# Expert matmuls on two 64-row tiles with two accumulations open at once, in an attention and mixture-of-experts kernel

## The chip, the cores and the metric

The kernel runs on one core of one Trainium2 chip. The metric is the device time of one execution in microseconds (us). Five engines work side by side: the TensorE (PE, with its weight loads shown apart as PEld), the VectorE (DVE), the ScalarE (ACT), GpSimd (POOL) and the SyncE (SP), whose queue issues most of the DMAs.

## The reference

What must be computed is attention with one key and value head for all sixteen query heads, followed by a mixture of experts with a choice in two stages. Cut to what matters:

```python
batch, n_heads, seq, head_dim = (8, 16, 384, 64)
scores = scale * np.matmul(q, k.transpose(0, 1, 3, 2))
attn = softmax(scores)
attn_out = np.matmul(attn, v)                       # (8, 16, 384, 64)
x = attn_out.transpose(0, 2, 1, 3).reshape(3072, 1024)
g_idx = argmax(x @ w_group)                         # 4 groups
e_idx = argmax(x_g @ w_expert[g])                   # 4 experts in a group
h = relu(x_e @ w1[g, e])                            # 1024 x 1024
out[tokens] = (g_w * e_w)[:, None] * (h @ w2[g, e]) # 1024 x 1024
```

All 384 tokens of a batch have nearly the same x, since the attention is nearly uniform, so that in seven of the eight batches all tokens go to one expert; in the last one 363 go to one and 21 to another.

## The kernel before

The work is cut into 96 steps. A step handles two units of two heads each, for one tile of 128 queries. Four steps make a tile t, three tiles (twelve steps) make a batch; this document calls these twelve steps a cycle and numbers the steps of a cycle 0 to 11, so step 16 of the program is step 4 of its cycle. The order in which each engine works is written out by hand: what an engine is given in the loop over `i` is what it does, in that order.

In each step:

- `scores` puts the scores of two units into PSUM. Each unit is two fp32 matmuls of 64 rows, one on the upper and one on the lower half of the array, into a bank each. Two such pairs of banks exist, so a unit waits until ACT has done with the same unit of the step before.
- `soft` lets DVE take the maximum (`nmx`) and ACT the exponential (`pr`) with its sum; `norm` lets DVE take the reciprocal and POOL multiply; `transp` lets DVE transpose the probabilities of the step before last into `ring`.
- In the steps with `p` 2 and 3 of a tile, `pv` multiplies with V for the tile before, on 32-row tiles into four banks `x`; after `p` 3, `pv_out` lets ACT copy the four banks to `xt`, and POOL cast them into the bf16 `xb`, from which the experts read.
- In the steps with `p` 0 and 1, the TensorE works on an expert. `expert` is a generator; `advance(groups)` lets it go on by so many accumulations of eight matmuls of 128 rows.

Besides, `logits` computes the logits of both stages on 32-column tiles, from the fp32 `xt`: for tile 0 of a batch in step 8 of its cycle, for tiles 1 and 2 in step 4 of the next. `logits_out` and `gate_masks` (DVE, one step later) turn them into masks. `gate_choose` counts, in a matmul with ones, for which expert the tokens of tile 0 vote, and `gate_pick` and `load_main` fetch the winner's weights (four DMAs that cast to bf16, issued by POOL in step 10). The expert of a batch begins in step 5 of the next cycle. Tokens that chose another expert are found at the end: the last batch has a second expert by plan, and a loop over a count read on the chip would run whatever is left.

All short-lived accumulations (pv, logits, the count, the experts) share four banks that `xbank()` gives out in turn; who takes a bank waits for whoever read it last. After the last step the score banks serve the experts too (`bank_end`).

The matmuls of an expert are 64 of 384 columns (`w1`, line 440, then a relu by ACT on line 446) and 48 of 512 columns (`w2`, line 454, then a scaled copy by ACT on line 472, and the stores by SP on line 498).

Of the kernel before, what the change touches and what calls it, by code (L numbers as in the profile page):

```python
# [19 lines left out]
def kernel(  # L20
# [11 lines left out]
    nc = tc.nc  # L32
    B, H, S, D = q.shape
# [5 lines left out]
    ST = S // P  # L39
    KO = Dm // P  # L40
    FO = F // P
    GE = G * Eg
# [25 lines left out]
    ident = singles.tile([P, P], FP32)  # L68
    make_identity(nc, ident)

    blank = singles.tile([P, 512], BF16)
    nc.vector.memset(blank[:], 0.0)

# [10 lines left out]
    st = {}  # L84
# [125 lines left out]
    def transp(u):  # L210

        nc.vector.transpose(  # L212
            out=ring[:, (u // 4) % 3, u % 4].rearrange("p h s -> p (h s)"),
            in_=st.pop(("pr", u))[:].rearrange("p h s -> p (h s)"),
        )
# [89 lines left out]
    def gate_choose(b):  # L305

        mask = st["g", b][1]
        c_ps = xbank()
        nc.tensor.matmul(
            out=c_ps[:, 0:GE], lhsT=ones[:], rhs=mask[:, 0].rearrange("p g e -> p (g e)"), start=True, stop=True  # L310
        )
        st["c_ps", b] = c_ps

# [116 lines left out]
    def keep_xb(b):  # L430
        nc.sync.dma_start(out=xb_dram[b], in_=st["xb", b][:].rearrange("p c t -> p (c t)"))

    def expert(xb, w1, w2, result, psum, on_act=None):

        on_act = on_act or (lambda k: k % 2 == 0)
        h_t = pool.tile([P, FO, S], BF16, tag="hT", bufs=1)
        for fc in range(FO):
            hp = psum()
            for ko in range(KO):
                nc.tensor.matmul(  # L440
                    out=hp[:, 0:S], lhsT=w1[:, ko, ts(fc, P)], rhs=xb[:, ko, :], start=(ko == 0), stop=(ko == KO - 1)
                )
                if ko % (KO // 2) == KO // 2 - 1:
                    yield
            if on_act(fc):
                nc.scalar.activation(out=h_t[:, fc, :], in_=hp[:, 0:S], func=ACTF.Relu)  # L446
            else:
                nc.vector.tensor_scalar(out=h_t[:, fc, :], in0=hp[:, 0:S], scalar1=0.0, scalar2=None, op0=ALU.max)
            yield
        for j in range(ST):  # L450
            for nh in range(2):
                yp = psum()
                for fo in range(FO):
                    nc.tensor.matmul(  # L454
                        out=yp, lhsT=h_t[:, fo, ts(j, P)], rhs=w2[:, fo, ts(nh, 512)],
                        start=(fo == 0), stop=(fo == FO - 1),
                    )
                    if fo % (FO // 2) == FO // 2 - 1:
                        yield
                result(j, nh, yp, on_act(FO + 2 * j + nh))  # L460
                yield

    def scaled(gcol, store):

# [60 lines left out]
    NT = B * ST  # L525
    pending = []

    def advance(groups):
        for _ in range(3 * groups):
# [19 lines left out]
    for b in range(B):  # L549
        s0 = SB * b  # L550
        for x, j0, j1 in ((s0 + 8, 0, 1), (s0 + 16, 1, ST)):
            at(x, "m2", logits, b, j0, j1)
            at(x + 1, "v", logits_out, b, j0, j1)
        for x, j0, j1 in ((s0 + 9, 0, 1), (s0 + 17, 1, ST)):
            at(x, "v", lambda b=b, j0=j0, j1=j1: st.__setitem__(("gm", b), gate_masks(b, j0, j1)))
            at(x, "v", lambda b=b: [next(st["gm", b]) for _ in range(3)])
        if b == 0:
            at(s0 + 10, "s", gate_choose, b)
            at(s0 + 10, "b", gate_score, b)
        else:  # L560
# [52 lines left out]
    load_v(0)  # L613
    for i in range(NSL):
        t, p = i // 4, i % 4
        if i >= SB + 5 and (i - 5) % SB == 0:
            pending.append(main_expert((i - 5) // SB - 1, lambda k: True))
        us = (2 * i, 2 * i + 1)
        for u in us:
            scores(u)  # L620
        run(i, "s")
        soft(us, lambda: run(i, "b"))
        if p < 2:
            run(i, "m0")
# [12 lines left out]
        run(i, "e")  # L637
        if p == 3 and t > 0:
            pv_out(t - 1)
        run(i, "g")  # L640
# [5 lines left out]
    st["ended"] = True  # L646
    transp(2 * i - 4)
    transp(2 * i - 3)
    advance(2)
    transp(2 * i - 2)  # L650
    transp(2 * i - 1)
    advance(2)
    run(i + 1, "w")
    advance(1)
    pv(NT - 1, 0, NB)
    pv_out(NT - 1)
    load_second(0)
    advance(2)
    run(i + 4, "m2")
    run(i + 4, "g")  # L660
    pending.append(main_expert(b, lambda k: k < FO or k % 2 == 0))
    advance(1)
# [102 lines left out]
```

## Time and profile before

| what | value |
|---|---|
| median of three runs | 530.9 us (530.18 to 537.23) |
| profiled execution | 532.53 us, its span 530.8 us |
| mean granted TensorE clock | 0.989 |
| TensorE busy | 502.5 us, 95% of the span |
| VectorE busy | 425.5 us, 80% |
| ScalarE busy | 319.2 us, 60% |
| GpSimd busy | 273.6 us, 52% |
| HBM | 101.79 MB read, 18.87 MB written |

A row of the timeline has the start, the length, the engine, the line, the operation, output<-inputs, shapes and count. `64*128` is the shape of the array's tile, rows by columns. The record of a matmul ends when its last result has left the array, so that the records of matmuls that follow each other overlap; the time of one is the distance between starts. An fp32 matmul stands as two rows. In brackets is the idle time of the engine ahead of the row, and what ended it.

### The profile page before, as it was taken

Reading aid. Unit: us, or ns where it says so; the run is one execution under the profiler, and the core shown is the slowest. Engines: PE = TensorE matmul, PEld = TensorE weight load, DVE = VectorE, ACT = ScalarE, POOL = GpSimd, SP = SyncE. Lnnn points to the kernel's source line nnn. Section 1 sums busy time; section 2 is a strip of 40 time slices with the busy share of each in tenths; the row PEclk is TensorE's granted clock in tenths of the full one; section 3 lists DMA queues with packets and bytes.
Section 4 is the critical chain, followed back from the end, with each engine's and each line's share of the span. In section 5 each row is a group of like instructions: output and inputs, shape, how many; then the busy total and the mean of one; then the engine's idle time right before and its main releaser. Section 6 shows DMA issues by size and latency. Waiting matters only on the chain.

```text
span 530.8 us, 18465 instructions
## 1 busy us (share of the span) xinstructions
PE 502.5 (95%) x7450; PEld 283.2 (53%) x7466; DVE 425.5 (80%) x825; ACT 319.2 (60%) x1005; POOL 273.6 (52%) x464
## 2 busy tenths in 40 slices
PE   6787899999999999999999999999999999999993
PEld 2254455555566556645555556645665555555451
DVE  2899988898899879998899878997999789914221
ACT  3676666677666766676576766676766666623210
POOL 1656854575565654485457546475358535613000
PEclk9799999999999999999999999999999999999998
DMA  7522699349963998379963996399946980199953
GB/s 119 123 43 43 122 239 217 72 82 224 262 151 63 212 250 226 72 125 237 272 133 61 223 251 166 72 186 233 270 81 105 232 232 2 26 230 259 212 117 96
DMA packets 64998, 84.14 MB, mean 159 GB/s; under 512 B 20496, under 2 KB 39952, under 8 KB 64912
## 3 DMA queue, kind: packets, MB, share of 16 engines
q0 software_dynamic: 19008, 37.75, 39.7%
q1 hardware_dynamic: 44720, 44.74, 32.1%
q8 instruction: 60, 0.98, 0.7%
q10 hardware_dynamic: 1184, 0.45, 0.4%
q14 instruction: 26, 0.21, 0.1%
HBM read 101.79 MB, written 18.87 MB: 227 GB/s over the span
## 4 chain that ended last, share of the span: by engine, by line
PE 79%; DVE 8%; DMA 6%; ACT 2%; issue 2%; POOL 1%; ACTq 0%; POOLq 0%; DVEq 0%
PE s L180 23%; PE x L228 23%; PE x L440 13%; PE x L454 12%; DMA w<-in_moe_w_dram 5%; PE sb L454 4%; DVE nmx L188 4%; DVE ring L212 3%; ACT pr L191 2%; PE sb L440 2%; PE x L251 2%; POOL pr L206 1%; DMA q_sb<-in_q_dram 1%; POOL w L415 0%; DVE rinv L202 0%
## 5 line engine op out<-in xcount | busy, mean ns | idle before, releaser
L206 POOL TENSOR_SCALAR pr<-pr,rinv 128x384 f32<-128x384 f32 x384 | 217.4, 586 | 193.8 <-DVE rinv L202 193.7
L191 ACT ACTIVATE pr<-s,nmx 128x384 f32<-128x384 f32 x384 | 217.7, 578 | 139.3 <-DVE nmx L188 131.5
L188 DVE TENSOR_REDUCE nmx<-s 128x2 f32<-128x768 f32 x192 | 174.0, 944 | 43.5 <-PE s L180 42.9
L212 DVE STREAM_TRANSPOSE ring<-pr 128x768 f32<-128x768 f32 x192 | 175.2, 951 | 0.1
L180 PE MATMUL s<-kt,qt 64*128 64x384 f32 x768 | 156.2, 520 | 11.8 <-ACT pr L191 11.7
L228 PE MATMUL x<-ring,v_sb 32*64 32x256 f32 x4608 | 140.1, 379 | 3.9 <-issue 2.8
L228 PEld LDWEIGHTS x<-ring,v_sb 32*64 32x64 f32 x4608 | 101.9, 131 | 45.7 <-issue 26.4
L180 PEld LDWEIGHTS s<-kt,qt 64*128 64x128 f32 x768 | 66.6, 189 | 71.9 <-ACT pr L191 36.0
L440 PEld LDWEIGHTS <-w 128*128 128x128 bf16 x576 | 54.5, 98 | 46.0 <-issue 11.4
L191 ACT ACTIVATION_READ_ACCUMULATOR pr<-s,nmx 128x1 f32 x384 | 77.8, 203 | 0.0
L440 PE MATMUL x<-xb,w 128*128 128x384 bf16 x448 | 76.4, 326 | 0.0
L454 PEld LDWEIGHTS <-h_t 128*128 128x128 bf16 x432 | 40.6, 98 | 56.9 <-issue 10.5
L454 PE MATMUL x<-w,h_t 128*128 128x512 bf16 x276 | 64.6, 380 | 0.6
L242 ACT COPY xt<-x 128x256 f32<-128x256 f32 x96 | 28.8, 392 | 8.9 <-PE x L228 8.9
L454 PE MATMUL sb<-w,h_t 128*128 128x512 bf16 x140 | 31.7, 379 | 0.3
L243 POOL CAST xb<-xt 128x1024 bf16<-128x1024 f32 x24 | 24.8, 1035 | 11.3 <-ACT xt L242 11.3
L446 ACT ACTIVATE h_t<-x 128x384 bf16<-128x384 f32 x56 | 25.2, 502 | 6.4 <-PE x L440 3.6
L415 POOL DMA_DIRECT2D w<-in_moe_w_dram x36 | 27.6, 780 | 0.3 <-issue 0.3
L170 DVE STREAM_TRANSPOSE qt<-q_sb 128x512 f32<-128x512 f32 x38 | 25.9, 682 | 0.0
L472 ACT ACTIVATE y<-x,gsel 128x512 f32<-128x512 f32 x36 | 24.3, 696 | 2.3 <-PE x L454 2.3
L440 PE MATMUL sb<-xb,w 128*128 128x384 bf16 x128 | 21.4, 326 | 0.0
L202 DVE RECIPROCAL rinv<-ssum 128x4 f32<-128x4 f32 x96 | 13.8, 144 | 3.1 <-ACT pr L191 3.1
(79 smaller groups left out, 139.3 us busy)
## 6 DMA issues: line engine op xcount, KB each, us to landing
w<-in_moe_w_dram POOLq DMA_DIRECT2D x36, 1024.0 KB, 19.5
q_sb<-in_q_dram SPq DMA_DIRECT2D x76, 224.0 KB, 6.3
out_dram<-y SPq DMA_DIRECT2D x84, 128.0 KB, 6.6
xb_scratch<-xb SPq DMA_DIRECT2D x8, 768.0 KB, 5.0
v_sb<-in_v_dram SPq DMA_DIRECT2D x32, 96.0 KB, 4.5
kk<-in_k_dram SPq DMA_DIRECT2D x30, 92.0 KB, 5.4
q_sb<-in_q_dram SPq DMA_DIRECT2D x16, 128.0 KB, 3.4
out_dram<-y SPq DMA_DIRECT2D x24, 64.0 KB, 1.7
```

Of the source, the lines that this page charges most:

```text
L170: nc.vector.transpose(out=qt[:].rearrange("p (x d) -> p x d", d=32), in_=q_sb[:, :, 0:32])
L180: nc.tensor.matmul(out=s[:, h, 0:S], lhsT=qt[r, ts(cc, P)], rhs=kt[r, :], start=True, stop=True)
L188: nc.vector.tensor_reduce(out=nmx[:], in_=s[:, :, 0:S], axis=AX.X, op=ALU.max, negate=True)
L191: nc.scalar.activation(out=pr[:, h, :], in_=s[:, h, 0:S], func=ACTF.Exp, bias=nmx[:, h:h + 1], scale=1.0, accum_out=ssum[:, k, h:h + 1],)
L206: nc.gpsimd.tensor_scalar(out=pr, in0=pr, scalar1=rinv[:, k, h:h + 1], scalar2=1.0, op0=ALU.mult, op1=ALU.mult)
L212: nc.vector.transpose(out=ring[:, (u // 4) % 3, u % 4].rearrange("p h s -> p (h s)"), in_=st.pop(("pr", u))[:].rearrange("p h s -> p (h s)"),)
L228: nc.tensor.matmul(out=o[i][h * D:(h + 1) * D, 0:2 * P].rearrange("d (g c q) -> d g c q", g=2, c=4), lhsT=v_sb[r, n, :], rhs=ring[r, a:z + ...
L242: nc.scalar.copy(out=xt[:, :, ts(i, 32)], in_=o[:, 0:2 * P].rearrange("p (c q) -> p c q", c=KO))
L415: nc.gpsimd.dma_start(out=w[:, o:o + 4, :], in_=(w1f, w2f)[n][ds(e, 1), :, o:o + 4, :].rearrange("o p c f -> (o p) c f"))
L440: nc.tensor.matmul(out=hp[:, 0:S], lhsT=w1[:, ko, ts(fc, P)], rhs=xb[:, ko, :], start=(ko == 0), stop=(ko == KO - 1))
L446: nc.scalar.activation(out=h_t[:, fc, :], in_=hp[:, 0:S], func=ACTF.Relu)
L454: nc.tensor.matmul(out=yp, lhsT=h_t[:, fo, ts(j, P)], rhs=w2[:, fo, ts(nh, 512)], start=(fo == 0), stop=(fo == FO - 1),)
```

## The change

The eight matmuls of 128 rows of one accumulation become sixteen matmuls of 64 rows. Two accumulations (a pair) are open at once, in two banks: for each of the eight slices of the contraction, the upper 64 rows go to one bank and the lower 64 rows to the other. That is one phase. In a second phase of the same pair the two halves change banks. Between the two phases of a pair stands a fence: a memset of one column on DVE that waits for the last matmul of the first phase, and for which the first matmul of the second phase waits. `fence()` is called right behind the scores of a step for all pairs that are open, and for one pair in the middle of a step where both its phases lie in that step.

An expert is fourteen phases in a fixed order, in which two pairs alternate: pairs 0 to 3 are `w1`, pairs 4 to 6 `w2`. `advance(phases)` now counts phases. They are spread as two in each of steps 4, 5, 8 and 9, and three in each of steps 0 and 1; before, the accumulations were spread as two in step 4, three in 5, two in 8, three in 9 and two in each of 0 and 1, of which those of step 4 belonged to the expert of the batch before. So an expert now begins in step 4 (step 16 of the program for the first) and ends in step 1. The logits come ahead of the expert's matmuls in steps 4 and 8 and are transposed in the same step. The count for the choice takes the 64 tokens in the lower partitions of tile 0 in place of 128. `bank_end` gives the two banks of a tile one after the other.

```diff
-            out=c_ps[:, 0:GE], lhsT=ones[:], rhs=mask[:, 0].rearrange("p g e -> p (g e)"), start=True, stop=True
+            out=c_ps[:, 0:GE], lhsT=ones[0:64, :], rhs=mask[0:64, 0].rearrange("p g e -> p (g e)"),
...
+    def fence(pairs=None):
+        pairs = list(unfenced) if pairs is None else pairs
+        if pairs:
+            f = nc.vector.memset(mark[:], 0.0)
+            tc.add_manual_dep(f.ins, [unfenced.pop(x) for x in pairs][-1].name, after, reason="banks change row tiles")
+            fenced.update(dict.fromkeys(pairs, f.ins))
...
-        for fc in range(FO):
-            hp = psum()
-            for ko in range(KO):
-                nc.tensor.matmul(
-                    out=hp[:, 0:S], lhsT=w1[:, ko, ts(fc, P)], rhs=xb[:, ko, :], start=(ko == 0), stop=(ko == KO - 1)
-                )
...
+        def phase(pair, swap):
+            ms = (2 * pair, 2 * pair + 1)
+            operands, n = (first, S) if ms[0] < FO else (second, 512)
+            if not swap:
+                banks[pair] = [psum() for _ in ms]
+            for c in range(KO):
+                for r in range(2):
+                    lhsT, rhs = operands(ms[r ^ swap], c, slice(64 * r, 64 * (r + 1)))
+                    mm = nc.tensor.matmul(
+                        out=banks[pair][r ^ swap][:, 0:n], lhsT=lhsT, rhs=rhs,
+                        start=(not swap and c == 0), stop=(swap == 1 and c == KO - 1),
+                    )
+                    if swap and c == 0 and r == 0:
+                        tc.add_manual_dep(mm.ins, fenced.pop(pair).name, after, reason="banks change row tiles")
+            if not swap:
+                unfenced[pair] = mm.ins
+            if swap:
+                for m, bank in zip(ms, banks.pop(pair)):
+                    evict(m, bank)
...
+        for pair, swap in (
+            (0, 0), (1, 0), (0, 1), (1, 1), (2, 0), (3, 0), (2, 1), (3, 1),
+            (4, 0), (5, 0), (4, 1), (6, 0), (5, 1), (6, 1),
+        ):
+            if swap and pair in unfenced:
+                for x in list(unfenced) if st.get("ended") else [pair]:
+                    fence([x])
+            phase(pair, swap)
             yield
...
-            free.extend(x[:, h, :] for h in range(2) for x in sb)
+            free.extend(x[:, h, :] for x in sb for h in range(2))
...
-            at(x, "m2", logits, b, j0, j1)
-            at(x + 1, "v", logits_out, b, j0, j1)
+            at(x, "m0", logits, b, j0, j1)
+            at(x, "v", logits_out, b, j0, j1)
...
-        if i >= SB + 5 and (i - 5) % SB == 0:
-            pending.append(main_expert((i - 5) // SB - 1, lambda k: True))
+        if i >= SB + 4 and (i - 4) % SB == 0:
+            pending.append(main_expert((i - 4) // SB - 1, lambda k: True))
...
+        fence()
         soft(us, lambda: run(i, "b"))
         if p < 2:
             run(i, "m0")
-            advance(1)
             run(i, "m1")
-            advance(2 if p == 1 and t % ST > 0 else 1)
+            advance(2)
...
         if i >= 2:
             transp(2 * i - 4)
+        if p < 2 and t % ST == 0:
+            advance(1)
+        if i >= 2:
             transp(2 * i - 3)
```

After the loop the remaining phases of the seventh expert, the eighth and the second one follow in the same way, with three, two and one phases around the last pv.

More of the change, by code (lines that the diff above doesn't have):

```diff
@@ L69 @@
     make_identity(nc, ident)
+    mark = singles.tile([P, 1], FP32)
     blank = singles.tile([P, 512], BF16)
@@ L309, in gate_choose @@
         nc.tensor.matmul(
-            out=c_ps[:, 0:GE], lhsT=ones[:], rhs=mask[:, 0].rearrange("p g e -> p (g e)"), start=True, stop=True
+            out=c_ps[:, 0:GE], lhsT=ones[0:64, :], rhs=mask[0:64, 0].rearrange("p g e -> p (g e)"),
+            start=True, stop=True,
         )
@@ L431, in keep_xb @@
         nc.sync.dma_start(out=xb_dram[b], in_=st["xb", b][:].rearrange("p c t -> p (c t)"))
+    after = mybir.DependencyInfo(mybir.DependencyClass.Sync, mybir.DependencyReason.DATA)
+    unfenced, fenced = {}, {}
+    def fence(pairs=None):
[4 more added lines that the diff above has]
+            fenced.update(dict.fromkeys(pairs, f.ins))
     def expert(xb, w1, w2, result, psum, on_act=None):
@@ L436, in expert @@
         h_t = pool.tile([P, FO, S], BF16, tag="hT", bufs=1)
-        for fc in range(FO):
-            hp = psum()
-            for ko in range(KO):
-                nc.tensor.matmul(
-                    out=hp[:, 0:S], lhsT=w1[:, ko, ts(fc, P)], rhs=xb[:, ko, :], start=(ko == 0), stop=(ko == KO - 1)
-                )
[L443 to L446, printed above, removed]
-            else:
-                nc.vector.tensor_scalar(out=h_t[:, fc, :], in0=hp[:, 0:S], scalar1=0.0, scalar2=None, op0=ALU.max)
-            yield
@@ L450, in expert @@
[L450 to L461, printed above, removed]
+        banks = {}
@@ new lines, in first, with second @@
+        def first(m, c, r):
+            return w1[r, c, ts(m, P)], xb[r, c, :]
+        def second(m, c, r):
+            j, nh = divmod(m - FO, 2)
+            return h_t[r, c, ts(j, P)], w2[r, c, ts(nh, 512)]
+        def phase(pair, swap):
[17 more added lines that the diff above has]
+                    evict(m, bank)
@@ new lines, in evict @@
+        def evict(m, bank):
+            if m >= FO:
+                result(*divmod(m - FO, 2), bank, on_act(m))
+            elif on_act(m):
+                nc.scalar.activation(out=h_t[:, m, :], in_=bank[:, 0:S], func=ACTF.Relu)
+            else:
+                nc.vector.tensor_scalar(out=h_t[:, m, :], in0=bank[:, 0:S], scalar1=0.0, scalar2=None, op0=ALU.max)
+        for pair, swap in (
[6 more added lines that the diff above has]
+            phase(pair, swap)
+            yield
@@ L526, with advance @@
     pending = []
-    def advance(groups):
-        for _ in range(3 * groups):
+    def advance(phases):
+        for _ in range(phases):
             while pending:
@@ L648 @@
     transp(2 * i - 3)
-    advance(2)
+    advance(3)
     transp(2 * i - 2)
     transp(2 * i - 1)
+    run(i + 1, "w")
     advance(2)
-    run(i + 1, "w")
-    advance(1)
     pv(NT - 1, 0, NB)
@@ L657 @@
     load_second(0)
-    advance(2)
-    run(i + 4, "m2")
+    advance(1)
+    run(i + 4, "m0")
+    run(i + 4, "v")
     run(i + 4, "g")
```

## The prediction

> **What bounds the kernel now.** I read the page first, then the order of the TensorE alone over one cycle of twelve steps, then the other engines at the places where the change puts something new. On the page, the second line gives busy time and the third what the chain that ended last is made of.
>
> ```profile
> span 530.8 us, 18465 instructions
> ...
> PE 502.5 (95%) x7450; PEld 283.2 (53%) x7466; DVE 425.5 (80%) x825; ACT 319.2 (60%) x1005; POOL 273.6 (52%) x464
> ...
> PE 79%; DVE 8%; DMA 6%; ACT 2%; issue 2%; POOL 1%; ACTq 0%; POOLq 0%; DVEq 0%
> ```
>
> So the TensorE sets the time. The columns of the next view are start, length, engine, line, tiles and count. I call the visits S (scores, L180), E (expert, L440 and L454), PV (L228), L (logits, L251) and G (the choice, L309), and number the steps 0 to 11 from 228.76 on; S0 is the start of step 0.
>
> ```profile
> 228.76 1.56 PE L180 MATMUL s<-kt,qt 64*128 64x384 f32 x8
> ...
> 247.40 1.56 PE L180 MATMUL s<-kt,qt 64*128 64x384 f32 x8
> 248.89 3.63 PE L454 MATMUL x<-w,h_t 128*128 128x512 bf16 x15
> 252.45 1.10 PE L251 MATMUL x<-xt,wge 128*32 128x64 f32 x64
> 253.48 1.56 PE L180 MATMUL s<-kt,qt 64*128 64x384 f32 x8
> 254.97 4.07 PE L440 MATMUL x<-xb,w 128*128 128x384 bf16 x24
> 258.97 1.56 PE L180 MATMUL s<-kt,qt 64*128 64x384 f32 x8
> 260.46 2.85 PE L228 MATMUL x<-ring,v_sb 32*64 32x256 f32 x96
> ...
> 267.51 1.56 PE L180 MATMUL s<-kt,qt 64*128 64x384 f32 x8
> 269.00 2.77 PE L440 MATMUL x<-xb,w 128*128 128x384 bf16 x16
> 271.70 0.76 PE L251 MATMUL x<-xt,wge 128*32 128x32 f32 x64
> 272.40 1.56 PE L180 MATMUL s<-kt,qt 64*128 64x384 f32 x8
> 273.89 4.07 PE L440 MATMUL x<-xb,w 128*128 128x384 bf16 x24
> 277.80 0.17 PE L309 MATMUL x<-mask_all,ones 128*128 128x16 bf16 x1
> ```
>
> Each visit starts before the record of the last has ended, so in these steps no other engine is waited for. What is left to save is the price of changing the tile shape. Twenty-four E matmuls followed by G, of the same 128-row shape, take 277.80 - 273.89 = 3.91 us, 0.163 each. Followed by S, of 64-row shape, they take 258.97 - 254.97 = 4.00. A change of shape costs 0.09. The view of line L180 by itself (shortest, median, longest duration in ns) gives the other part:
>
> ```profile
> L180 PEld LDWEIGHTS s<-kt,qt x32: 183/186/187, 259.0 to 273.2; 64*128 64x128 f32 x32
> L180 PE MATMUL s<-kt,qt x32: 482/482/587, 259.0 to 273.5; 64*128 64x384 f32 x32
> ```
>
> The first pass of a visit is 0.105 longer than the rest: its weights have to be loaded with nothing streaming, after the change of shape. The other three passes add (1.56 - 0.587)/3 = 0.324 each, so S is 1.30 of streaming. S is also the form of the new E: two 64-row tiles at once, one bank each.
>
> **The change part by part: what it saves.** In the new kernel S, E and G all have 64 rows. Between S and E neither change remains: 0.09 into E, and 0.09 + 0.105 into the next S, 0.29 per visit in steps 0, 1, 5 and 9. In steps 4 and 8 the logits now stand between S and E, so two changes stay and only 0.09 + 0.105 goes. Sum 4 x 0.29 + 2 x 0.195 = 1.55 us per cycle, or 10 us over the six and a half cycles in which experts run. Bounds: nothing, if a bf16 tile after an fp32 tile still drains, and this 10.
>
> **The new matmuls.** Two 64-row matmuls take the place of one of 128 rows. No row shows bf16 at 64 rows. If the two tiles stream side by side, as those of S do, the cost is nothing; if one after the other, it is the whole E time again: 9 experts x 112 x about 0.186 (0.163 for 64 of them, 0.216 for the 48 of 512 columns) = 187 us. I take nothing, since the S rows are the nearest. Weight loads are twice as many, and the row of the old ones is
>
> ```profile
> L440 PEld LDWEIGHTS <-w 128*128 128x128 bf16 x576 | 54.5, 98 | 46.0 <-issue 11.4
> ```
>
> If each pair's load were in the open, that would be 9 x 112 x 0.098 = 99 us. S speaks against it: only its first load of four shows. The Trainium skill, page "TensorE: Matmul & The Clock Gate", Part 3, The mechanism, has it that a weight load overlaps a running matmul only if the two lie in different row groups. By that rule each row tile would wait for its own loads and the 99 us would be due; the S rows, where the second, third and fourth load of the same row group hide, disagree, and I go by them.
>
> **The earlier start: xb.** The expert's first pair now comes in step 4, right behind the logits, and reads the whole of xb, whose last third POOL casts in that very step:
>
> ```profile
> 247.81 2.26 POOL L206 TENSOR_SCALAR pr<-pr,rinv 128x384 f32<-128x384 f32 x4 [2.00 <-DVE rinv L202]
> 248.36 1.82 DVE L188 TENSOR_REDUCE nmx<-s 128x2 f32<-128x768 f32 x2 [0.64 <-PE s L180]
> 250.02 1.04 POOL L243 CAST xb<-xt 128x1024 bf16<-128x1024 f32 x1
> ```
>
> The cast stands behind the four normalisations and ends at 251.06, 3.66 after the step's start. The TensorE is there after S (1.30 + 0.105), a change (0.09) and L (253.48 - 252.45 = 1.03, its own change in it): 2.52. The old kernel did not care: in step 4 it still ran the previous expert. Wait 1.15 plus a handover: 1.2, in seven cycles 8.4 us. S of step 5 stands behind it. Bounds 1.0 and 1.3.
>
> **G and the h_t evictions.** The four x banks go round in turn. In step 9 the first two phases close, and G takes the bank that pair 2's first relu frees. ACT has that relu behind the step's four exponentials. The old kernel's rows for this chain:
>
> ```profile
> 272.62 0.67 DVE L170 STREAM_TRANSPOSE qt<-q_sb 128x512 f32<-128x512 f32 x1
> 273.36 1.82 DVE L188 TENSOR_REDUCE nmx<-s 128x2 f32<-128x768 f32 x2
> 275.10 0.21 DVE L261 STREAM_TRANSPOSE lg<-x 128x32 f32<-128x32 f32 x1
> 276.65 0.88 ACT L446 ACTIVATE h_t<-x 128x384 bf16<-128x384 f32 x2
> ```
>
> From the maximum to the end of the first relu it is 276.65 + 0.50 - 273.36 = 3.79 (two relus 0.88, so one is about 0.50). In the old kernel G needed no such bank. In the new step 9 the maximum starts at the earliest 0.86 after S begins to stream (272.40 to 273.36 less the 0.105), so the bank is free at 4.65; the TensorE arrives at 1.30 + 16 x 0.163 = 3.91. DVE closes step 8 with the row of 272.62, 5.78 after that step's start (267.51); with the logits' transpose (0.21) and a fence of 0.06 it is 6.05, where S of step 9 begins at 1.40 + 0.09 + 0.70 + 2.61 = 4.80 and its maximum could start at 5.66: 0.4 later. Wait 0.75 to 1.2; I take 1.1, 7.7 us in seven cycles. S of step 10 is queued behind G.
>
> **Step 5, DVE.** E of this step shrinks from 24 matmuls to the equal of 16, but DVE's work stays:
>
> ```profile
> 254.44 1.82 DVE L188 TENSOR_REDUCE nmx<-s 128x2 f32<-128x768 f32 x2 [1.86 <-PE s L180]
> 256.18 0.24 DVE L261 STREAM_TRANSPOSE lg<-x 128x64 f32<-128x64 f32 x1
> 257.79 1.83 DVE L212 STREAM_TRANSPOSE ring<-pr 128x768 f32<-128x768 f32 x2
> ```
>
> The transposes that PV of step 6 reads end at 259.62, 5.18 after the maximum began, or 4.94 without the logits' transpose. In the new step that is 0.86 + 4.94 = 5.80 after S begins; PV could start at 1.30 + 2.61 + 1.30 + 0.09 = 5.30. Wait 0.5, and S of step 7, which takes over a score bank that ACT frees late by the same backlog, perhaps 0.3: together 0.8, 5.6 us in seven cycles. Bounds 0 and 1.
>
> **Steps 0 and 1, now three phases each.** The fences are memsets of about 0.06, and these are the nearest rows for them, for DVE's start in step 0 and for a y copy:
>
> ```profile
> L606 DVE MEMSET iota<- 128x1 f32 x16 | 0.6, 59 | 0.0
> 230.73 1.79 DVE L188 TENSOR_REDUCE nmx<-s 128x2 f32<-128x768 f32 x2
> L472 ACT ACTIVATE y<-x,gsel 128x512 f32<-128x512 f32 x36 | 24.3, 696 | 2.3 <-PE x L454 2.3
> ```
>
> Three of the five per cycle stand ahead of the maxima, where DVE waits for S anyway, and are hidden. The other two, for pairs 4 and 6, stand between the two ring transposes. Pair 4's stands behind two maxima (1.79) and one transpose (0.91). DVE comes to step 0 1.97 late (230.73 - 228.76), so the memset is done at 4.73, and the TensorE wants it after 1.40 + 2 x 1.73 = 4.86: just hidden; with the backlog of steps 8 to 11 half a microsecond larger, 0.3 in the open. What waits behind it on DVE is the second transpose, wanted only two steps on. Pair 6 takes the banks that two y copies of 0.70 free, about 1.3 after pair 4 closes, with S (1.30) as cover and 0.2 for the last result to land: 0.25. PV of step 2 takes those of pair 6: 0.15. In all 0.7 in six cycles, 4.2 us; bounds 0 and 1.2.
>
> **The end.** Here no S is between the phases. Pair 6 opens right when pair 4 has closed and needs both its banks: 0.2 plus one or two evictions of 0.70 or 0.75, that is 1.0 to 1.6, for three experts 4 us. The last phase closes two results together:
>
> ```profile
> 514.41 12.57 SPq L515 DMA_DIRECT2D out_dram<-y  x24
> 522.20 0.75 DVE L510 SCALAR_TENSOR_TENSOR y<-sb,gsel,y 128x512 f32<-128x512 f32 x1 [0.91 <-PE sb L454]
> ```
>
> SP issues a store in 12.57/24 = 0.52; the last four results now come bunched, and eight stores, where four were, stand behind the last matmul: 2 us. The two counts of the last batch keep 128 rows and now sit between 64-row phases: 0.4. Sum 6.4, bounds 2 and 9.
>
> **The choice by 64 tokens** halves G's rows and not its time; the same experts win in every batch, so no left-over expert is run.
>
> **Sum.** -10 + 8.4 + 7.7 + 5.6 + 4.2 + 6.4 = +22.3. On the profiled execution's own 532.5 that is 554.8; that execution lies 1.6 above the median, so against the median of 530.9 I say 553. A measurement tells about 2% from no change: 520.3 and 541.5 are the limits.
>
> **Rivals.** First, not slower: the longer steps 0 and 1 let DVE, ACT and POOL catch up, so that cast, relus and transposes stand ready when the TensorE comes to steps 4 to 11. For it: the other engines are under 80%. Against: DVE already idles before the maxima of steps 4 and 5 (0.64 and 1.86 in the rows of 248.36 and 254.44), so there is no backlog to lose, and the queues of POOL and ACT are the same. It decides from the point where the cast ends by 2.5 after the start of step 4. It takes 8.4 + 7.7 + 5.6 away: 531. Second, the change does not do what it says: a bf16 tile after an fp32 one still drains, and the 10 us are not saved: 563. For it: no row shows the two types in one shape following each other. Third, weight loads or row tiles do not overlap: 652 or 740, against which the S rows stand.
>
> **How the numbers follow.** Forecast 0.63, its own range 541 to 564; not slower 0.13; no saving 0.16; no overlap 0.05; gain unhidden, with waits and end at their low bounds, below 520, 0.03. Range 534 to 570: it leaves out the overlap case and the tails. Same takes the not-slower rival and the forecast's low tail, 0.15; faster 0.03; slower 0.82.
>
> **What would show it.** Right: no gap between S and E; E pairs 0.163 and 0.216 apart; an idle TensorE of about 1.2 in step 4 ended by POOL's cast, about 1 in step 9 ended by a relu, half of one in step 6 ended by the ring transpose; a cycle of 59 to 61 instead of 57.68. Wrong: a cycle under 57, or E pairs wider than these.

## The result, and the profile after

The changed kernel takes 563.8 us (median of four runs, 563.3 to 566.5), where the kernel before takes 532.2 beside it: 1.059 times as long, with a 95% interval of 1.0505 to 1.0675. It is slower, as forecast, and lies 11 us above the predicted 553, inside the range of 534 to 570. The profiled execution took 564.24 us with a span of 562.8 at a granted clock of 0.988.

The page after, the same three lines as before:

```profile
span 562.8 us, 20510 instructions
...
PE 507.1 (90%) x8474; PEld 303.4 (54%) x8474; DVE 424.9 (76%) x874; ACT 318.7 (57%) x1005; POOL 273.8 (49%) x464
...
PE 61%; DVE 17%; ACT 9%; POOL 4%; issue 4%; DMA 2%; ACTq 0%; DVEq 0%
```

The TensorE is busy for about as long as before (502.5, now 507.1) in a span that is 32 us longer, and on the chain that ended last it went from 79% to 61%, DVE from 8% to 17%. So 27 of the 32 us are time in which the TensorE stands idle. Where it waits stands in the view of TensorE waits, by the tile and line that wait, who ended the wait, the sum in us, the number of waits and the longest:

```profile
PE s L181 <- ACT pr L192: 8.6, 15, 1.6
PE sb L468 <- DVE mark L442: 6.7, 4, 3.2
PE x L310 <- ACT h_t L484: 4.1, 6, 0.7
PE x L468 <- POOL xb L244: 3.8, 7, 1.1
PE x L229 <- issue: 3.7, 4, 1.7
PE x L229 <- ACT h_t L484: 3.0, 6, 0.5
```

L468 is E, L310 is G, L229 PV, L181 S and L252 L in the numbering of the changed kernel; `mark` is what the fence writes. The first line is no part of the difference: these waits lie in the first two cycles, and the kernel before has 11.7 us of them there. One cycle in the timeline of the TensorE:

```profile
294.37 1.75 PE L181 MATMUL s<-kt,qt 64*128 64x384 f32 x8
295.95 5.44 PE L468 MATMUL x<-w,h_t 64*128 64x512 bf16 x48
301.23 1.45 PE L181 MATMUL s<-kt,qt 64*128 64x384 f32 x8
302.51 5.57 PE L468 MATMUL x<-w,h_t 64*128 64x512 bf16 x48
307.73 1.65 PE L181 MATMUL s<-kt,qt 64*128 64x384 f32 x8
...
317.22 1.56 PE L181 MATMUL s<-kt,qt 64*128 64x384 f32 x8
...
320.16 2.77 PE L468 MATMUL x<-xb,w 64*128 64x384 bf16 x32 [0.35 <-POOL xb L244]
322.76 1.55 PE L181 MATMUL s<-kt,qt 64*128 64x384 f32 x8
324.14 2.77 PE L468 MATMUL x<-xb,w 64*128 64x384 bf16 x32
326.74 1.46 PE L181 MATMUL s<-kt,qt 64*128 64x384 f32 x8
328.70 3.26 PE L229 MATMUL x<-ring,v_sb 32*64 32x256 f32 x96 [0.51 <-ACT h_t L484]
...
341.03 1.45 PE L181 MATMUL s<-kt,qt 64*128 64x384 f32 x8
342.32 2.76 PE L468 MATMUL x<-xb,w 64*128 64x384 bf16 x32
345.79 0.17 PE L310 MATMUL x<-mask_all,ones 64*128 64x16 bf16 x1 [0.71 <-ACT h_t L484]
345.80 1.55 PE L181 MATMUL s<-kt,qt 64*128 64x384 f32 x8
347.29 2.85 PE L229 MATMUL x<-ring,v_sb 32*64 32x256 f32 x96
```

Steps 0 and 1 are 6.86 and 6.50 long (from one S to the next), step 4 is 5.54, step 9 (from 341.03) is 4.77. The whole cycle, from this S to that of 354.37, is 60.0, against 57.67 before. To split the loop from the end, take the start of the last step of the loop, step 95, in both kernels; first before, then after:

```profile
456.95 1.56 PE L180 MATMUL s<-kt,qt 64*128 64x384 f32 x8
```

```profile
472.89 1.56 PE L181 MATMUL s<-kt,qt 64*128 64x384 f32 x8
```

Up to there the change costs 15.9 us. From there to the end of the span it was 530.8 - 456.95 = 73.9 and is 562.8 - 472.89 = 89.9: the end costs another 16.1. The waits of the end, in the timelines of the TensorE, of DVE and of SP's queue:

```profile
483.87 3.63 PE L468 MATMUL sb<-w,h_t 64*128 64x512 bf16 x32 [1.36 <-ACT y L508]
...
509.58 2.77 PE L468 MATMUL sb<-xb,w 64*128 64x384 bf16 x32 [3.23 <-DVE mark L442]
...
519.15 3.63 PE L468 MATMUL sb<-w,h_t 64*128 64x512 bf16 x32 [1.62 <-DVE y L510]
524.42 1.90 PE L468 MATMUL sb<-w,h_t 64*128 64x512 bf16 x16 [1.64 <-DVE mark L442]
...
544.05 3.63 PE L468 MATMUL sb<-w,h_t 64*128 64x512 bf16 x32 [1.50 <-DVE y L546]
549.21 1.90 PE L468 MATMUL sb<-w,h_t 64*128 64x512 bf16 x16 [1.53 <-DVE mark L442]
```

```profile
506.39 0.29 DVE L739 CAST lsi<-x 128x128 int32<-128x128 f32 x1 [2.76 <-PE x L737]
...
509.46 0.19 DVE L442 MEMSET mark<- 128x1 f32 x2
...
523.59 0.75 DVE L510 TENSOR_SCALAR y<-sb,gsel 128x512 f32<-128x512 f32 x1 [4.49 <-ACT y L508]
524.29 0.06 DVE L442 MEMSET mark<- 128x1 f32 x1
```

```profile
543.36 15.60 SPq L551 DMA_DIRECT2D out_dram<-y  x24
```

Two kinds of waits are seen. The bank waits (1.36, 1.62, 1.50) are the first phase of pair 6, which needs both banks of pair 4 right when pair 4 has closed. The waits on `mark` are the fence itself: a memset of 0.06 that stands in DVE's queue behind other work. At 509.46 that is 3 us of the gate's arithmetic, at 524.29 the y eviction of pair 5.

### The profile page after: what moved, and what is told of

The parts are those of the page before. It is cut to its first block, busy times and chain, and to the rows that moved or that the text cites. A ratio compares the mean times of both kernels' runs of the same rounds, so it can differ in the third digit from the quotient of the medians.

```text
span 562.8 us, 20510 instructions
## 1 busy us (share of the span) xinstructions
PE 507.1 (90%) x8474; PEld 303.4 (54%) x8474; DVE 424.9 (76%) x874; ACT 318.7 (57%) x1005; POOL 273.8 (49%) x464
## 4 chain that ended last, share of the span: by engine, by line
PE 61%; DVE 17%; ACT 9%; POOL 4%; issue 4%; DMA 2%; ACTq 0%; DVEq 0%
PE x L229 21%; PE s L181 16%; PE x L468 15%; PE sb L468 9%; DVE nmx L189 8%; ACT pr L192 6%; DVE ring L213 5%; POOL pr L207 3%; ACT h_t L484 2%; DMA xb_scratch<-xb 1%; POOL xb L244 1%; DVE y L546 1%; DMA q_sb<-in_q_dram 1%; DVE qt L171 1%; ACT y L508 1%
## 5 line engine op out<-in xcount | busy, mean ns | idle before, releaser
L181 PE MATMUL s<-kt,qt 64*128 64x384 f32 x768 | 157.1, 518 | 10.4 <-ACT pr L192 8.6
L229 PE MATMUL x<-ring,v_sb 32*64 32x256 f32 x4608 | 143.7, 379 | 8.1 <-issue 3.7
L229 PEld LDWEIGHTS x<-ring,v_sb 32*64 32x64 f32 x4608 | 109.2, 131 | 47.0 <-issue 20.6
L181 PEld LDWEIGHTS s<-kt,qt 64*128 64x128 f32 x768 | 70.9, 190 | 69.9 <-ACT pr L192 41.0
L468 PEld LDWEIGHTS <-w 64*128 64x128 bf16 x1152 | 59.1, 94 | 46.7 <-issue 8.5
L468 PE MATMUL x<-xb,w 64*128 64x384 bf16 x896 | 78.6, 323 | 5.9 <-POOL xb L244 3.8
L468 PEld LDWEIGHTS <-h_t 64*128 64x128 bf16 x864 | 44.7, 94 | 60.4 <-issue 9.8
L468 PE MATMUL x<-w,h_t 64*128 64x512 bf16 x576 | 66.0, 376 | 0.0
L468 PE MATMUL sb<-w,h_t 64*128 64x512 bf16 x288 | 32.6, 376 | 7.6 <-DVE mark L442 3.2
L508 ACT ACTIVATE y<-x,gsel 128x512 f32<-128x512 f32 x36 | 22.8, 684 | 16.1 <-PE x L468 16.1
L468 PE MATMUL sb<-xb,w 64*128 64x384 bf16 x256 | 21.8, 323 | 3.5 <-DVE mark L442 3.5
L442 DVE MEMSET mark<- 128x1 f32 x49 | 2.9, 59 | 22.9 <-PE sb L468 14.8
```

Source lines behind the costliest of these rows:

```text
L181: nc.tensor.matmul(out=s[:, h, 0:S], lhsT=qt[r, ts(cc, P)], rhs=kt[r, :], start=True, stop=True)
L229: nc.tensor.matmul(out=o[i][h * D:(h + 1) * D, 0:2 * P].rearrange("d (g c q) -> d g c q", g=2, c=4), lhsT=v_sb[r, n, :], rhs=ring[r, a:z + ...
L468: mm = nc.tensor.matmul(out=banks[pair][r ^ swap][:, 0:n], lhsT=lhsT, rhs=rhs, start=(not swap and c == 0), stop=(swap == 1 and c == KO - 1),)
L508: nc.scalar.activation(out=y[:, ts(nh, 512)], in_=yp, func=ACTF.Copy, scale=g)
```

## The experiments

Two theories. W: the row tiles cost nothing by themselves; the time is in waits that the new order of work, the pairs and the fences make. R: the row tiles themselves, with their doubled matmuls and loads, are what costs. Each run is compared with runs of the kernel before on the same chip (531.9 to 532.8).

**The cast ahead of the normalising, in all tiles.**

```diff
+        if p == 3 and t > 0:
+            pv_out(t - 1)
         norm(us)
         run(i, "e")
-        if p == 3 and t > 0:
-            pv_out(t - 1)
```

> Edit: the changed kernel, with pv_out (ACT's copies and POOL's cast of xb) given out ahead of norm in the steps with p 3, so that POOL casts before it normalises. Theory W (the time goes into waits of the TensorE that the new schedule makes; row tiles themselves cost nothing): the expert in step 4 no longer waits for the cast, which then ends about 2.4 after the step's start against the TensorE's 2.5; step 4 becomes 5.1 to 5.2 in all cycles, and the kernel 4 to 8 us faster than the changed one (556 to 560, ratio to the kernel before 1.045 to 1.052). Theory R (the row tiles themselves, with double the instructions and loads and the fences, make the expert slower): nothing over 2 us.

Measured: 580.2 us, 1.080 [1.068, 1.092], a miss on the wrong side. Step 4 did become 5.13 in cycles 2 to 4 (the first cycle is cycle 0), so its wait was the cast; in cycles 5 to 7 it is 6.34 to 8.82, with pauses of up to 2.1 in which nothing is waited for. But the reorder also moved the casts of the other two tiles. Step 0 went from 6.86 to 8.42; the first row is in its middle, in the timeline of the TensorE, the other two are ahead of it, in those of DVE and POOL:

```profile
181.29 1.90 PE L468 MATMUL x<-w,h_t 64*128 64x512 bf16 x16 [1.51 <-DVE mark L442]
```

```profile
176.75 1.80 DVE L406 TENSOR_TENSOR grem_all<-gate,gs 128x48 f32<-128x48 f32 x1
177.37 1.09 POOL L244 CAST xb<-xt 128x1024 bf16<-128x1024 f32 x1
```

DVE comes to its subtraction on L406 2.14 after the start of the step, no later than in the changed kernel (2.16). There it takes 0.21; here, in all six such steps, it takes 1.80 and ends 0.09 after POOL's cast. All that DVE does behind it, the fence too, is late by 1.57. Why the two end together was not tried. The rest of the loss is in step 9 (5.28 instead of 4.77) and in the pauses. What follows: the fence inside step 0 had no slack left, as the prediction had it, and only the cast of step 3 may be moved.

**The cast ahead of the normalising, in step 3 of the cycle alone.**

```diff
+        early = p == 3 and t > 0 and t % ST == 0
+        if early:
+            pv_out(t - 1)
         norm(us)
         run(i, "e")
-        if p == 3 and t > 0:
+        if p == 3 and t > 0 and not early:
             pv_out(t - 1)
```

> The changed kernel, with the cast of xb put ahead of the normalizing only in step 3 of a cycle (the last 128-token tile of a batch, the only cast that an expert phase of the next step waits for). W (the time lies in waits that the new schedule, the pairs and the fences make): step 4 falls from 6.31 to about 5.1 us where the cast was waited for and by 0.4 where it wasn't, steps 0 and 9 stay at 6.86 and 4.77, because the casts of the other tiles stand where they stood: 4 to 8 us less, 556 to 560. R (the row tiles themselves cost the time): no change, 563 to 565. The rival inside W is that the normalizing of step 3, now behind the cast, makes a later step wait: then step 5 or 6 grows by what step 4 loses, 563 or more.

Measured: 560.9 us, 1.0523 [1.0472, 1.0573], 3 us under the changed kernel; the two intervals overlap, so the time alone does not tell them apart. The steps do: 0 and 9 are untouched, no wait on the cast is left, and step 4 is 5.13 in cycles 2 to 4, as these rows of one of them show (253.71 to 258.84):

```profile
253.71 1.56 PE L181 MATMUL s<-kt,qt 64*128 64x384 f32 x8
...
256.23 2.77 PE L468 MATMUL x<-xb,w 64*128 64x384 bf16 x32
258.84 1.45 PE L181 MATMUL s<-kt,qt 64*128 64x384 f32 x8
```

In cycles 5 to 7 the gain is lost again inside E, with nothing waited for:

```profile
378.67 1.15 PE L468 MATMUL x<-xb,w 64*128 64x384 bf16 x12 [1.20 <-issue]
```

So the wait on the cast is real, and its removal is worth some 3 us (steps 3 and 4 together gain 1.2, 0.8 and 0.6 in cycles 2 to 4), not the 8 that seven waits of 1.2 would give.

**The choice one step later.**

```diff
-        if b == 0:
-            at(s0 + 10, "s", gate_choose, b)
-            at(s0 + 10, "b", gate_score, b)
-        else:
-            at(s0 + 9, "m2", gate_choose, b)
-            at(s0 + 9, "w", gate_score, b)
+        at(s0 + 10, "s", gate_choose, b)
+        at(s0 + 10, "b", gate_score, b)
```

> Edit: the changed kernel, with the count for the choice moved for all batches from the end of step 9 to behind the scores of step 10, as batch 0 has it, and its reading by DVE to step 10. Theory W: the 0.83 that the TensorE idles in step 9 for a relu goes; S of step 10 starts right behind E, step 9 becomes 3.9 and step 10 stays under 4.6, together 0.5 to 0.9 less per cycle, 3 to 6 us in all (558 to 561). A rival within W: the wait only moves to the pv of step 10, which needs four banks, and nothing is won. Theory R: no change.

Measured: 567.9 us, 1.063 [1.055, 1.072]. Step 9 fell from 4.77 to 3.89, the wait of G is gone, but step 10 rose from 4.26 to 6.1. G's bank is one of the four that PV takes, and now DVE has to read the count in front of PV (second row):

```profile
348.52 0.77 PE L229 MATMUL x<-ring,v_sb 32*64 32x256 f32 x12 [0.42 <-DVE rinv L203]
350.01 2.81 PE L229 MATMUL x<-ring,v_sb 32*64 32x256 f32 x84 [0.71 <-DVE scr L319]
```

The inner rival was right: the wait moves, and grows.

**The end on 128 rows.** The two experts of the last batch as in the kernel before, one accumulation at a time, the rest as changed.

```diff
-        yield from expert(st["xb", b], w1, w2, scaled(...), any_bank, on_act)
+        yield from (expert_rows128 if b == B - 1 else expert)(st["xb", b], w1, w2, scaled(...), any_bank, on_act)
...
-        yield from expert(st["xb", b], *st.pop("w_second"), result, any_bank, on_act)
+        yield from expert_rows128(st["xb", b], *st.pop("w_second"), result, any_bank, on_act)
```

> Edit: the changed kernel, with the two experts of the last batch on 128 rows, one accumulation at a time, without fences; all else as changed. Theory W: the five idle stretches of the TensorE of 1.5 to 3.2 in these two experts and the longer tail go, 11 to 15 us (549 to 553). Theory R: two of nine experts are undone, 2/9 of 32, 7 us (557).

Measured: 560.7 us, 1.0525 [1.0444, 1.0606], a miss: only 3 us less. The fences are gone, but other waits stand in their place, in the groups of TensorE instructions (busy us, mean ns, then the idle time before them and who ended it):

```profile
L506 PE MATMUL sb<-xb,w 128*128 128x384 bf16 x128 | 22.6, 326 | 4.7 <-ACT h_t L510 4.7
L518 PE MATMUL sb<-w,h_t 128*128 128x512 bf16 x94 | 21.9, 379 | 5.1 <-DVE y L572 2.5 <-ACT y L534 2.5
```

The edit left `bank_end` as changed, which gives the two banks of one PSUM tile one after the other. Every second accumulation then waited 0.58 to 0.84 for the eviction of the other bank of its tile, 9.8 us in all. The run had changed two things at once; the next one mends that.

**The end on 128 rows, with its banks in turn from the two tiles.** These lines come on top of those of the run before.

```diff
-            free.extend(x[:, h, :] for x in sb for h in range(2))
+            if st.get("rows128"):
+                free.extend(x[:, h, :] for h in range(2) for x in sb)
+            else:
+                free.extend(x[:, h, :] for x in sb for h in range(2))
...
+    st["rows128"] = True
     pending.append(main_expert(b, lambda k: k < FO or k % 2 == 0))
```

> The changed kernel, with the two experts of the last batch on 128 rows, no pairs or fences there, and the banks of those two taken in turn from the two PSUM tiles, as in the kernel before (the run with the 128-row end alone took them one tile after the other and waited 0.58 to 0.84 us for every second bank). W: from the start of step 95 to the end the time comes near that of the kernel before, 74 to 78 instead of 89.9, so 549 to 553 in all. The rival is that the pairs of the seventh expert, which stay, and the matmuls themselves hold half of the end's surplus: 555 to 558.

Measured: 550.9 us, 1.0345 [1.0282, 1.0409]. From step 95 to the end it takes 77.5 instead of 89.9, and the experts of the last batch run without a wait from this row on:

```profile
507.60 10.52 PE L518 MATMUL sb<-w,h_t 128*128 128x512 bf16 x47
```

So 12.4 of the 16.1 us of the end are pairs and fences of the last batch's two experts. What stays is the pair 6 of the seventh expert (1.36), a wait of 0.64 for a relu, 0.9 more behind the last matmul, and 0.7 of a pause in PV, which is 1.91 here and 1.20 in the kernel before.

**The fences of the end given out earlier.**

```diff
             phase(pair, swap)
+            if pair == 6 and not swap and st.get("ended"):
+                fence()
             yield
...
     advance(3)
+    fence()
     ls_ps = xbank()
```

> The changed kernel, with the fences of the end given out earlier: that of pair 6 straight behind its first phase, ahead of the y evictions of pair 5 on VectorE, and those of pairs 2 and 3 of the eighth expert straight behind their first phases, ahead of the gate's work on VectorE. W: the three waits on the mark in the trace of after, 3.23 + 1.64 + 1.53 = 6.4 us, fall to some 0.3 together, and nothing else follows the chain at once, so the end loses 5 to 6 us: 558 to 559. R: the fences' waits would be replaced by others of the same size (the banks of pair 6, at 1.4 to 1.6 each, or the gate's work, which now stands behind the fences): under 2 us less, 562 to 564.

Measured: 556.3 us, 1.044 [1.037, 1.051]. The end takes 83.3, 6.6 less. The phase behind the count (first row) and the second phase of pair 6 (the last 16 matmuls of the second row) wait for no fence now; the bank waits stand as before:

```profile
504.48 2.77 PE L468 MATMUL sb<-xb,w 64*128 64x384 bf16 x32
...
514.05 5.36 PE L468 MATMUL sb<-w,h_t 64*128 64x512 bf16 x48 [1.62 <-DVE y L512]
```

Two calls of `fence()` were put in, so that the memsets are given out earlier, and nothing else was changed; 0.4 of the 6.6 is a shorter pause in PV. The place of the memsets in DVE's queue was 6 us of the end.

**The new order of work without row tiles.** Every expert as one accumulation over 128 rows after the other, no pairs, no fences, banks in turn, choice by 128 tokens; the steps as changed.

```diff
-            out=c_ps[:, 0:GE], lhsT=ones[0:64, :], rhs=mask[0:64, 0].rearrange("p g e -> p (g e)"),
+            out=c_ps[:, 0:GE], lhsT=ones[:], rhs=mask[:, 0].rearrange("p g e -> p (g e)"),
...
-        yield from expert(st["xb", b], w1, w2, scaled(...), any_bank, on_act)
+        yield from expert_rows128(st["xb", b], w1, w2, scaled(...), any_bank, on_act)
```

> Edit: the changed schedule (start in step 4, two, two, two, two, three, three phases, logits ahead) but every phase is one accumulation of eight 128-row matmuls, without fences and without pairs; the choice by 128 tokens. Theory W: the shape changes come back (plus 10), the waits that pairs and fences make go (G, the banks of pairs, the whole end: minus 23 to 25), the wait for the cast in step 4 stays: 548 to 552. Theory R: the row tiles are the cost, so this is near the kernel before, 531 to 537.

Measured: 547.9 us, 1.0268 [1.0192, 1.0345], at the lower edge of what W said and far from R's 537. It sorts W into places. Step 95 begins at 472.1, where it began at 472.9 with row tiles, and at 470.9 to 471.4 in the three runs above that changed the end alone: over the whole loop row tiles gain or lose no more than about 1 us. The end is 74.5: without pairs and fences it is close to the 73.9 of the kernel before. In the cycle of these rows step 4 has the whole wait, since nothing ahead of it pauses:

```profile
318.67 1.10 PE L252 MATMUL x<-xt,wge 128*32 128x64 f32 x64
320.89 2.76 PE L506 MATMUL x<-xb,w 128*128 128x384 bf16 x16 [1.12 <-POOL xb L244]
```

The order of work alone costs 15 us in the loop: in a cycle step 4 waits 1.1, and steps 6, 7, 10 and 11 are 4.70, 4.59, 4.43 and 4.75 instead of 4.27, 1.4 in sum.

**A version with the phases spread.** Row tiles and pairs, but two phases in each of steps 0, 1, 4 and 5, three in each of 8 and 9; each expert's first pair in steps 4 and 5 stands behind pair 6 of the expert before; fences behind their phase; the end on 128 rows with banks in turn.

```diff
-            (0, 0), (1, 0), (0, 1), (1, 1), (2, 0), (3, 0), (2, 1), (3, 1),
-            (4, 0), (5, 0), (4, 1), (6, 0), (5, 1), (6, 1),
+            (0, 0), (0, 1), (1, 0), (2, 0), (1, 1), (3, 0), (2, 1), (3, 1),
+            (4, 0), (5, 0), (4, 1), (5, 1), (6, 0), (6, 1),
...
-            advance(2)
+            c = i % SB
+            if c in (4, 5):
+                for x in pending[:2]:
+                    next(x)
...
+            else:
+                advance(3 if c in (8, 9) else 2)
```

> A version of its own: row tiles and pairs as in the changed kernel, but the phases spread over the steps as evenly as in the kernel before, 2 in steps 0, 1, 4 and 5, 3 in steps 8 and 9; the new expert's first phase in step 4 stands behind the old expert's phase (6,0), which covers the cast of xb, and its second in step 5 behind (6,1); fences inside a step stand straight behind the phase that they close; the last batch's experts run on 128 rows with banks in turn. W: steps 0 and 1 fall to about 4.8 each, 4 to 5.8, 5 to about 4, 8 and 9 come to 5.9 and 5.2, the PV steps stay at 4.3: a cycle of 56 instead of 59.9 and of 57.67 in the kernel before; with an end of 75 to 78 that gives 520 to 530. R: with the loads and instructions doubled the cycle stays at 58 or more: 536 to 550.

Measured: 542.1 us, 1.0153 [1.0097, 1.0209]: better than the change by 22 us, but not than the kernel before: a miss for W, whose range ended at 530, and inside the range of R. Step 95 begins at 463.9, the end takes 76.6. Steps 0 to 11 are 4.91, 5.07, 4.89, 4.27, 5.56, 4.32, 4.66, 4.41, 6.43, 5.22, 4.29, 4.27 where nothing pauses, 58.3 a cycle and not 56. Two pairs that close together leave four evictions to ACT in a row, and PV of step 2 takes 3.58 instead of 2.85. ACT's timeline and the TensorE's:

```profile
301.55 2.43 ACT L535 ACTIVATE y<-x,gsel 128x512 f32<-128x512 f32 x4
```

```profile
303.26 3.58 PE L229 MATMUL x<-ring,v_sb 32*64 32x256 f32 x96
```

**The spread version on 128 rows.**

```diff
-        yield from (expert_rows128 if b == B - 1 else expert)(st["xb", b], w1, w2, scaled(...), any_bank, on_act)
+        yield from expert_rows128(st["xb", b], w1, w2, scaled(...), any_bank, on_act)
```

> The spread version (542.1 us, step 95 starts at 463.9) with every expert phase as one accumulation over 128 rows: no pairs, no fences, no row tiles, choice by 128 tokens, banks of the end in turn; the order of the phases stays. It says what row tiles and pairs bring in one and the same order of work. In the trace of the spread version the row tiles save 0.14 to 0.3 us a change of shape, some 0.8 a cycle in steps 0, 1, 4, 5 and 9, and the pairs' evictions, which come two and two ahead of a PV step, cost 0.62 in step 2, 0.39 in step 6, 0.14 in step 7. W: both go away together, a cycle of 57.7 to 58.2 instead of 58.3 and 533 to 540 in all. R, that doubled instructions and loads of the row tiles cost: 531 or less. The other rival, that the row tiles do save their 1.5 a cycle and something else in this order is late: 546 or more.

The choice is by 128 tokens here too. It asks whether the missing 12 us are the row tiles' own cost. Measured: 545.4 us, 1.0217 [1.0166, 1.0269], a miss for W, on the side of the rival that the row tiles do save, and short of its 546. Steps 0 to 11 are 5.05, 5.05, 4.27, 4.27, 5.66, 5.10, 4.82, 4.27, 6.19, 5.51, 4.27, 4.27, in sum 58.7. Against the spread version the pairs save 0.14 in step 0, 0.10 in 4, 0.78 in 5, 0.16 in 6 and 0.29 in 9, and lose 0.62 in step 2, 0.14 in 7, 0.24 in 8: 0.4 a cycle to the good, 3 us in all, and the intervals of the two overlap. (Step 95 of the two profiled executions begins 6.4 apart; most of the rest is pauses, 8.2 in all here and 5.7 in the spread version.) In step 5 the 0.78 is more than a change of shape: on 128 rows S of step 6 waits for ACT there.

```profile
325.79 0.92 PE L181 MATMUL s<-kt,qt 64*128 64x384 f32 x4 [0.41 <-ACT pr L192]
```

That ends R, though its range had held the run before: where the order of work is the same, row tiles are as fast or a little faster, in both orders that were tried. What keeps the spread version behind the kernel before is read from its steps alone: the heap of evictions ahead of step 2, and the longer steps 6 and 8, which it has on 128 rows too. Why these are longer was not tried further. No version that was run beats the kernel before.

## Why the prediction was right, point by point, and where it was not

**The loop: predicted 15.9, measured 15.9.** Without the end, the terms of the sum are -10 + 8.4 + 7.7 + 5.6 + 4.2 = +15.9, and step 95 begins 15.9 later. That the two agree to the tenth is luck: in the three runs that changed the end alone step 95 begins 13.9 to 14.5 later. The size is not luck alone, since a cycle is 60.0 where it was 57.67, and the terms make 2.25 a cycle. But some terms err against each other: G cost less than forecast, while the saving was smaller and the PV steps cost more.

- *Row tiles side by side, loads hidden: right.* In the cycle above 32 matmuls, two phases, take 326.74 - 324.14 = 2.60, 0.163 for each two that run side by side, and 48 of the second layer 307.73 - 302.51 = 5.22, 0.218: the same as the single matmuls of 128 rows (0.163 and 0.216). The Trainium skill, page "TensorE: Matmul & The Clock Gate", Part 3, The mechanism, in its list of what overlaps, lets a weight load overlap a running matmul only in another row group. By that rule the 99 us would have been due; the trace disagrees with it, since the matmuls follow each other at the distances above.
- *No change of shape between S and E: right, a little too large.* Step 9 has S at 341.03 and E at 342.32, 1.29 apart, which is the streaming of S alone. So a bf16 tile does follow an fp32 tile of the same shape without a drain, and the rival "no saving" falls by its mechanism, though its 563 is the time that came. Step 5 is 3.89 in most cycles (4.20 with the same phases on 128 rows), 0.31 saved, where 0.29 was forecast. Steps 4 and 8 show 0.09 each: step 8 is 4.80 (before 4.89), and step 4 without its wait 5.13, where two smaller accumulations would leave 6.08 - 2 x (1.73 - 1.30) = 5.22 of the old step. The other 0.105 of their 0.195 comes in the S behind them. It is not saved in step 10, where S behind G takes 347.29 - 345.80 = 1.49, as S ahead of PV did before.
- *xb in step 4: the mechanism right, the sum too large.* The wait is 1.1 where step 3 runs undisturbed, as the run on 128 rows shows. But in most cycles an unforeseen pause inside step 3 or 4 takes up the same time: in cycles 2 to 5 step 3 is 4.27, 4.41, 4.91 and 5.04 long and step 4 is 6.31, 6.17, 5.67 and 5.54, in sum 10.58 each time. So the view of waits has 3.8 us in seven waits, and taking the wait away gave 3, not 8.4.
- *G behind the relu: right, smaller.* 0.65 to 0.71 a time, six times, ended by the relu as described, against 1.1; 4.1 plus one wait of 0.9 for the ring, not 7.7.
- *PV of step 6: the size right, the reason wrong.* The wait is 0.5 as forecast, but what ends it is the relu that frees PV's bank (ACT, `h_t`), not the ring transpose of DVE. Steps 6 and 7 together are 1.0 a cycle longer than before, against the 0.8 forecast.
- *Steps 0 and 1: right within their bounds.* 13.36 in the two, where the same phases on 128 rows take 13.75: they save 0.39. Of the 0.58 forecast 0.105 would come in the S of step 2, and most of the rest goes to the fence: E is 301.23 - 295.95 = 5.28 long in step 0 and 5.22 in step 1. The run with all casts moved shows how thin the cover of pair 4's fence is: DVE was 1.6 later there, and the TensorE waited 1.51. In the loop pair 6 waits for its banks hardly at all; step 2 is 4.45 where it was 4.27, 0.18 against the 0.15 forecast.

**The end: predicted 6.4, measured 16.1. This is the step that failed.** Its own items came out near: the banks of pair 6 1.36 + 1.62 + 1.50 = 4.5 against 4, and from the end of the last matmul (549.21 + 1.90) to the end of the span it is 11.7, where before it was 530.8 - (514.66 + 7.50) = 8.6, so 3 against 2 for the stores: SP's row has 15.60 for the 24 of them, where it had 12.57. The last matmuls of the kernel before:

```profile
514.66 7.50 PE L454 MATMUL sb<-w,h_t 128*128 128x512 bf16 x34
```

What was left out is the fence. The prediction costed the fences for steps 0 and 1, where it asked what stands ahead of them on DVE, and never asked it for the end. There they wait behind the gate's arithmetic and the y evictions, 3.23 + 1.64 + 1.53 + 0.32 = 6.7. Giving them out earlier took some 6 off the end, and taking out the pairs of the last batch 12.4. With that term the sum would have been +29, against a median that is 31.7 higher.

**The rivals.** "Not slower" needed the cast to end by 2.5 after the start of step 4; in the cycle shown, where step 4 starts at 317.22 and step 3 had paused, it ends at 320.11, 2.9 after, in the timeline of POOL:

```profile
319.07 1.04 POOL L244 CAST xb<-xt 128x1024 bf16<-128x1024 f32 x1
```

The longer steps 0 and 1 didn't help it. "No overlap" is excluded by the pitch of the pairs.

## What to carry to other kernels

A synchronising instruction that costs 0.06 costs what stands ahead of it in its queue: wherever a fence is put, list that queue at every place where it will be given out, the end of the program too. When several results close together instead of one after the other, their evictions come in a heap, and whoever takes all of those banks next pays for it. And a gain in the matmuls (0.3 per visit of an expert here) is only kept if the order of work around it stays as even as it was: the order alone cost 15 us in this loop.

## What the runs showed of the hardware that was not expected

The TensorE pauses with nothing in the profile that it waits for ("issue"). In the changed kernel the longest are 1.69 in the PV of step 7 of cycle 1 and 1.54 in the PV of the end; the kernel before pauses at the same two places, for 1.23 and 1.20. Others move from kernel to kernel: up to 0.9 in the PV of step 3 and 0.98 in E of step 4 in the changed kernel, up to 1.30 in E of step 4 in the version with the cast of step 3 moved. The page's table of DMA queues has a queue, q8, that brings instructions in packets while the kernel runs (before: 60 packets; below, after):

```profile
q8 instruction: 69, 1.13, 0.8%
```

The two runs whose experts are all on 128 rows have 60 packets as well, those with row tiles 66 to 69. The eleven traces have 82 pauses of over 0.15 us that end in "issue". 81 of them end 1.2 to 1.6 us after the end of a packet of q8, and these packets are 6.4 to 7.3 us apart in the median, so that chance would put about one pause in fifteen there. In the changed kernel, for one, a packet is under way from 492.18 to 493.16, and the pause in the PV of the end lasts from 492.84 to 494.38. So the pauses go with the fetch of instructions. But most packets bring no pause (60 packets and three pauses in the kernel before), and no run changed the fetching by itself, so it stays open what makes a packet come too late. What is shown besides is that such a pause can swallow a wait of the same size in the next step, as the 10.58 of steps 3 and 4 has it.
